# Three weight conversions tied to other marks, and one division moved to ScalarE, in a fused attention and FNet kernel

## The chip, the cores and the metric

The kernel runs on one core of a Trainium2 chip. TensorE (PE) multiplies, VectorE (DVE) and ScalarE (ACT) read its results from PSUM and write SBUF, GpSimd (POOL) helps a little, and SyncE (SP) issues nearly all the DMAs. The metric is the time on the device in microseconds (us), the median of several runs. One more execution was profiled; all rows below are from it.

## The reference

```
scores_l = scale * q @ k.T, masked to |i - j| < 16
scores_s = scale * q @ k_sum.T + log(32)       # k_sum: maxima over blocks of 32 keys
a = softmax(concat(scores_l, scores_s));  x = a @ concat(v, v_sum)   # v_sum: block means
x -> (4 batches, 768 tokens, 512 channels)
u  = x + real(fft2(x));   un = (u - mean) / sqrt(var + 1e-6)
out = u + relu(un @ w_ch1) @ w_ch2             # 512 -> 2048 -> 512
```

q, k, v have 4 batches, 8 heads, 768 tokens and 64 channels per head. The two weights arrive as float64, and the kernel turns them into float32 itself.

## The kernel before, in words

The four batches are worked one after the other, and the attention of batch b + 1 runs in the gaps of the two layers of batch b. Heads go in four pairs g = 0..3. For a pair, `scores` and `sum_scores` make the scores (tiles `sc`, `ss`) and their exponentials `p` on ScalarE; `values` multiplies them with the values into two PSUM banks `av`, whose last column is the sum of the exponentials, takes the reciprocal (`rec`), and multiplies the rest by it into `x` (for the tokens of batch 1 the tile is `x_919`, for those of batch 0 `x_145`). `prepare` transposes the next pair's q and k on TensorE (tiles `qk`) and ScalarE copies them out.

The two layers use a Strassen-like scheme: seven products instead of eight. `gen_hidden(b, c)` is the first layer, half c of the 16 column blocks: four steps j (0 to 3 for c = 0, 4 to 7 for c = 1), seven products each, in three banks `hx`, `hy`, `hz`, with left factors from a tile `w` of seven 128-column parts (four of the weight, three sums of them). Its result is the tile `h`. `gen_out(b, c)` is the second layer on that half: three rows i of token blocks, seven products each, in banks `ox`, `oy`, `oz`. VectorE adds every product to `x`; such an addition is a *join*. In `gen_out(0, 0)` the first row is done plainly: two tiles of 128 tokens (t = 0 and t = 3, banks `o`), one join each, while the right-hand sums of `w_ch2` (`w_0_0` to `w_0_3`) are still being formed.

`gen_weights` converts the weights during batch 0. One piece is one call of `make(f, j)`: f = 1 a column block of `w_ch1`, f = 2 a row block of `w_ch2`. The pieces go in the order of `plan`, and each piece's raw words are loaded into the tile `words`, which has room for two pieces. `convert` takes, on VectorE, five instructions of 128x1024 (exponent bits, mantissa bits, sign, scaled low word, product), on ScalarE two (exponent, mantissa), and then `_left_sums` or `_right_sums` adds three smaller ones on VectorE; the finished tile is stored to DRAM (`dw`) for the later batches. The third entry of a plan line is a stage. The generator goes on when this stage is in `issued`, and if `marks` has an instruction under that name, the piece's instructions are put behind that instruction by the scheduler (`tc.issue_after`). The stages `("h", 0, j)` are in `issued` only: they hold the generator back but name no instruction.

The order on each engine is set by a scheduler from the order of the code, its priorities and `issue_after`. PE, DVE, ACT and the DMA queue of SP each work through their own list.

Four PSUM banks serve `hx`..`oz` and `o`, and four more serve the attention. A product can start when the bank it gets has been read out by the join or the copy that used it last.

Of the kernel before, what the change touches and what calls it, by code (L numbers as in the profile page):

```python
# [12 lines left out]
AF = mybir.ActivationFunctionType  # L13
# [3 lines left out]
P = 128  # L17
# [479 lines left out]
def _main_program(ctx, tc, q, k, v, moe_w_ch1, moe_w_ch2, out):  # L497


    nc = tc.nc  # L500
    B, H, S, D = q.shape
    DM = H * D
    DF = moe_w_ch1.shape[1]
    NST = S // P
# [9 lines left out]
    HT = NST // 2  # L514
# [5 lines left out]
    ADD, SUB = ALU.add, ALU.subtract  # L520
# [39 lines left out]
    def fetch(out, in_):  # L560

        ins = nc.sync.dma_start(out=out, in_=in_)
        if in_order[0]:
            tc.keep_in_program_order(ins)
        return ins.ins

    def abank(shape, name):
        return psum.tile(shape, FP, tag="attn", bufs=4, name=name)

    def bank(shape, name):  # L570
        return psum.tile(shape, FP, tag="bank", bufs=4, name=name)
# [9 lines left out]
    def tt(out, in0, in1, op):  # L581
        return nc.vector.tensor_tensor(out=out, in0=in0, in1=in1, op=op).ins  # L582
# [5 lines left out]
    nat, marks = {}, {}  # L588
# [249 lines left out]
    def values(b, g, p, pm, x):  # L838
        vw = vw_bufs[g % 2]
        av = [abank([P, NST, D1], f"av_{b}_{g}_{r}") for r in range(2)]  # L840
        for t in range(NST):
            h = t // HT
            for j in range(4):
                for r in range(2):
                    rows, i = slice(64 * r, 64 * (r + 1)), 4 * t + j
                    nc.tensor.matmul(av[r][32 * j:32 * (j + 1), t, :], p[rows, h, i - NB2 * h, :], vw[rows, i, :],
                                     start=(t == 0), stop=False, skip_group_check=True)
        for t in range(HT):
            for r in range(2):
                rows = slice(64 * r, 64 * (r + 1))  # L850
                ins = nc.tensor.matmul(av[r][:, t:t + HT + 1:HT, :], pm[rows, P * t:P * (t + 1)], vs[rows],
                                       start=False, stop=(t == HT - 1), skip_group_check=True)
        marks["av", b, g] = ins.ins
        for r in range(2):
            rc = rec[:, b * NP + g, r]
            nc.vector.reciprocal(out=rc, in_=av[r][:, :, D])
            xo = x[:, 0, P * g + D * r:P * g + D * (r + 1)]
            xo = bass.AP(xo.tensor, xo.offset, [list(xo.ap[0]), [HT * DM + D * (1 - 2 * r), 2], [DM, HT], [1, D]])
            tt(xo, av[r].rearrange("p (h t) d -> p h t d", h=2)[:, :, :, 0:D],
               rc.rearrange("p (h t) -> p h t", h=2)[:, :, :, None].to_broadcast([P, 2, HT, D]), ALU.mult)  # L860
# [208 lines left out]
    def gen_attention(b):  # L1069
# [13 lines left out]
        for g in range(NP + 1):  # L1083
# [6 lines left out]
            if past:  # L1090
                if b > 1:
                    scale_sums(b, g - 1)
                values(b, g - 1, *past, x)
                if n1 and b > 1:
                    load_values(*n1)
# [50 lines left out]
    wt, issued = {}, set()  # L1146
# [1 line left out]


    plan = [(1, 0, ("fold", 0)), (1, 1, ("mx", 0)), (1, 2, ("mx", 0)), (2, 0, ("sums", 0)), (1, 3, ("h", 0, 0)), (2, 1, ("mx", 0)),  # L1150
            (2, 2, ("mx", 0)), (2, 3, ("mx", 0)), (1, 4, ("h", 0, 1)), (1, 5, ("h", 0, 2)), (1, 6, ("h", 0, 3)),
            (2, 4, ("o", 0, 0)), (1, 7, ("h", 0, 4))] + [(2, j, ("o", 0, 0)) for j in range(5, NJ)]
    pieces = [(f, j, hh) for f, j, _ in plan for hh in range(2)]
    raws, stores = [], []
# [354 lines left out]
    def one_sum(b, c, i):  # L1509

        if i and queue.get("last"):
            with tc.issue_after(marks["dense"]):
                for part in queue["last"].pop(0):
                    tt(*part)
# [192 lines left out]
    def gen_out(b, c):  # L1707
        x, h = x_of[b], wt["h", b]
        js = range(NC * c, NC * (c + 1))
        plain = (0, HT) if (b, c) == (0, 0) else ()  # L1710
        if plain:
            for t in plain:
                for j in js[0:2] if t == 0 else js[2:4]:
                    w = wt[2, 0, j]
                    tt(w[:, T1], w[:, B12], w[:, B11], SUB)
                    tt(w[:, T2], w[:, B22], w[:, T1], SUB)
                    tt(w[:, T4], w[:, B21], w[:, T2], SUB)
                ps = bank([P, DM], f"o_{b}_{c}_{t}")
                for n, j in enumerate(js):
                    for hf in range(2):  # L1720
                        nc.tensor.matmul(ps, h[:, n, hf, P * t:P * (t + 1)], wt[2, b, j][:, 2 * hf:2 * hf + 2, :],
                                         start=(n, hf) == (0, 0), stop=(n, hf) == (NC - 1, 1))
                    if n % 2 == 0:
                        yield
                tt(x[:, t, :], ps, x[:, t, :], ADD)
            for j in js:
                w = wt[2, 0, j]
                tt(w[:, T3], w[:, B22], w[:, B12], SUB)
                fetch(out=dw2[j][:, 1:7], in_=w[:, 1:7])
        for i in range(1 if plain else 0, HT):  # L1730
            t1, t2 = slice(P * i, P * (i + 1)), slice(S2 + P * i, S2 + P * (i + 1))
            left = {A11: h[:, :, 0, t1], A12: h[:, :, 1, t1], A22: h[:, :, 1, t2]}
            for s in (S1, S2_, S3, S4):
                left[s] = bpool.tile([P, NC, P], FP, tag="s", bufs=5, name=f"s{s}_{b}_{c}_{i}")
            a21 = h[:, :, 0, t2]
            tt(left[S1], a21, left[A22], ADD)
            tt(left[S2_], left[S1], left[A11], SUB)
            tt(left[S3], left[A11], a21, SUB)
            tt(left[S4], left[A12], left[S2_], SUB)
            X, Y, Z = (bank([P, HD], f"o{n}_{b}_{c}_{i}") for n in "xyz")  # L1740
            x11, x12 = x[:, i, 0:HD], x[:, i, HD:DM]
            x21, x22 = x[:, HT + i, 0:HD], x[:, HT + i, HD:DM]

            def product(ps, a, r, start, stop):
                for n, j in enumerate(js):
                    nc.tensor.matmul(ps, left[a][:, n, :], wt[2, b, j][:, r, :], start=start and n == 0,  # L1746
                                     stop=stop and n == NC - 1, skip_group_check=True)

            def join(*a):
                marks["dense"] = tt(*a)  # L1750
                if (b, c) == (B - 2, 1) and i:
                    joins.append(marks["dense"])

            product(X, A11, B11, True, False)
            join(x11, X, x11, ADD)
            product(Y, A12, B21, True, True)
            join(x11, Y, x11, ADD)
            one_sum(b, c, i)
            yield
            product(X, S2_, T2, False, False)  # L1760
            join(x12, X, x12, ADD)
            product(Z, S1, T1, True, False)
            join(x22, Z, x22, ADD)
            one_sum(b, c, i)
            yield
            product(X, S3, T3, False, False)
            join(x22, X, x22, ADD)
            last = (b, c, i) == (B - 1, 1, HT - 1)
            if last:
                fetch(out=out[b, P * (HT + i):P * (HT + i + 1), HD:DM], in_=x22)  # L1770
            product(Z, S4, B22, False, True)
            join(x12, Z, x12, ADD)
            if last:
                fetch(out=out[b, P * i:P * (i + 1), :], in_=x[:, i, :])
            one_sum(b, c, i)
            yield
            product(X, A22, T4, False, True)
            join(x21, X, x21, ADD)
            if NC * (c + 1) == NJ and not last:
                for t in (i, HT + i):  # L1780
                    fetch(out=out[b, P * t:P * (t + 1), :], in_=x[:, t, :])
            elif last:
                fetch(out=out[b, P * (HT + i):P * (HT + i + 1), 0:HD], in_=x21)
            if i == HT - 1:
                issued.add(("o", b, c))
            one_sum(b, c, i)
            yield
# [8 lines left out]
    ps = bank([P, 512], "warm")  # L1796
# [14 lines left out]
    for vw in vw_bufs + [third]:  # L1811
        nc.gpsimd.tensor_copy(out=vw[:, :, D].rearrange("p (e n) -> p e n", e=2),
                              in_=count[:, None, :].to_broadcast([P, 2, NQ]))
# [52 lines left out]
    for b in range(B):  # L1866
# [20 lines left out]
        if b == B - 2:  # L1887
# [9 lines left out]
            ps = bank([1, 1], "flag_ps")  # L1897
# [5 lines left out]
def kernel(tc, q, k, v, moe_w_ch1, moe_w_ch2, out):  # L1903
    nc = tc.nc
    with ExitStack() as ctx:
        flag = _main_program(ctx, tc, q, k, v, moe_w_ch1, moe_w_ch2, out)
        redo = nc.values_load(flag[0:1, 0:1], min_val=0, max_val=1)
    with tc.If(redo > 0):
        _general_program(tc, q, k, v, moe_w_ch1, moe_w_ch2, out)
# [30 lines left out]
```

## Time and profile before

| what | value |
|---|---|
| median of 3 runs | 794.03 us (792.45 to 794.19) |
| the profiled execution | 794.12 us, span 792.3 us |
| PE busy | 767.6 us (97%) |
| DVE busy | 541.1 us (68%) |
| ACT busy | 248.9 us (31%) |
| DMA | 120.36 MB, 152 GB/s mean |

Times in rows count from the start of the span. The profiled execution's time is 1.8 us more than its span, and 0.1 us above the median. Busy times of PE contain waiting inside its pipeline, so the waits, the clock and the distances between neighbouring rows say more than the share. Batch 0's layers, the conversions and batch 1's attention lie between about 86 and 240 us; after that the later batches follow.

### The profile page before, as it was taken

What the parts mean: (1) busy time and instruction counts of PE and PEld (TensorE: products, weight loads), DVE (VectorE), ACT (ScalarE), POOL (GpSimd) and SP (SyncE); (2) the same over time, 40 slices, a digit from 0 to 9 for tenths busy, and PEclk for the clock granted to TensorE, in tenths of its full rate; (3) what the DMA queues carried; (4) which work ended last, traced back from release to release, by engine and by line L of the source; (5) the groups of instructions that cost most, each with busy time, mean ns of one, the idle gap of its engine ahead of it and who ended that gap; (6) DMA issues with size and microseconds to landing.
All of it is one profiled execution on the core that took longest, in us unless ns stands there. A gap on an engine that the chain in (4) does not pass through costs nothing.

```text
span 792.3 us, 14996 instructions
## 1 busy us (share of the span) xinstructions
PE 767.6 (97%) x6068; PEld 591.0 (75%) x6068; DVE 541.1 (68%) x1145; ACT 248.9 (31%) x579; POOL 74.3 (9%) x102
## 2 busy tenths in 40 slices
PE   8999999869999999999999999999999999999997
PEld 5777555557569876688669876688659889889986
DVE  4789999976988825464576726463476987756762
ACT  3755657232535212200126112210116214203300
POOL 1000000000000002300030002300030004201500
PEclk8999999969999999999999999999999999999999
DMA  9897879695884359966244149820614034204001
GB/s 201 227 247 176 182 239 259 204 271 195 223 220 143 92 172 244 182 97 161 93 183 153 41 147 200 220 95 27 251 48 156 27 145 188 93 1 186 0 29 57
DMA packets 135901, 120.36 MB, mean 152 GB/s; under 512 B 94512, under 2 KB 117904, under 8 KB 135824
## 3 DMA queue, kind: packets, MB, share of 16 engines
q1 hardware_dynamic: 134672, 117.05, 53.6%
q0 software_dynamic: 576, 2.10, 0.8%
q8 instruction: 50, 0.82, 0.4%
q10 hardware_dynamic: 576, 0.17, 0.1%
q14 instruction: 27, 0.22, 0.1%
HBM read 97.28 MB, written 22.02 MB: 151 GB/s over the span
## 4 chain that ended last, share of the span: by engine, by line
PE 80%; DVE 12%; ACT 3%; DMA 2%; issue 1%; SPq 0%; DVEq 0%
PE ox L1746 19%; PE hx L1450 13%; PE oz L1746 10%; PE hz L1450 6%; PE oy L1746 5%; PE t L1619 4%; PE hy L1450 3%; PE y L1323 3%; DVE w L582 2%; PE f L1619 2%; PE mx L1282 2%; DMA words<-in_moe_w_ch_dram 2%; PE sc L810 2%; DVE w L1192 2%; PE sc L750 1%
## 5 line engine op out<-in xcount | busy, mean ns | idle before, releaser
L1450 PE MATMUL hx<-u,w 128*128 128x384 f32 x384 | 139.8, 492 | 1.2 <-ACT h L1461 0.8
L1450 PEld LDWEIGHTS hx<-u,w 128*128 128x128 f32 x384 | 71.1, 190 | 52.9 <-ACT p L817 3.7
L1746 PE MATMUL ox<-w,h 128*128 128x256 f32 x368 | 87.5, 382 | 4.1 <-DVE x L582 4.1
L1746 PE MATMUL ox<-w,s 128*128 128x256 f32 x368 | 89.3, 385 | 0.0
L1746 PE MATMUL oz<-w,s 128*128 128x256 f32 x368 | 89.0, 380 | 0.0
L1746 PEld LDWEIGHTS ox<-w,h 128*128 128x128 f32 x368 | 69.5, 191 | 16.1 <-DVE x L582 4.3
L1746 PEld LDWEIGHTS ox<-w,s 128*128 128x128 f32 x368 | 70.2, 193 | 10.6 <-DVE x L582 0.8
L582 DVE TENSOR_TENSOR x<-ox,x 128x256 f32<-128x256 f32 x92 | 38.9, 423 | 56.3 <-PE ox L1746 56.0
L1746 PEld LDWEIGHTS oz<-w,s 128*128 128x128 f32 x368 | 69.6, 190 | 9.5 <-DVE x L582 0.4
L1450 PE MATMUL hz<-u,w 128*128 128x384 f32 x192 | 70.3, 488 | 0.1
L1450 PEld LDWEIGHTS hz<-u,w 128*128 128x128 f32 x192 | 36.4, 190 | 25.6 <-DVE u L582 0.7
L1461 ACT COPY h<-hx 128x384 f32<-128x384 f32 x24 | 11.4, 476 | 114.0 <-PE hx L1450 114.0
L1746 PE MATMUL oy<-w,h 128*128 128x256 f32 x184 | 44.3, 381 | 0.7 <-ACT h L1668 0.7
L1622 ACT COPY f<-t 128x192 f32<-128x192 f32 x52 | 15.8, 303 | 78.3 <-PE t L1619 78.1
L582 DVE TENSOR_TENSOR x<-oz,x 128x256 f32<-128x256 f32 x46 | 19.5, 423 | 29.4 <-PE oz L1746 29.1
L1746 PEld LDWEIGHTS oy<-w,h 128*128 128x128 f32 x184 | 34.7, 190 | 6.2 <-ACT h L1668 1.5
L1598 POOL TENSOR_SCALAR h<-h 128x768 f32<-128x768 f32 x12 | 25.4, 2127 | 137.5 <-DVE h L1578 137.5
L585 POOL TENSOR_TENSOR vb<-vb 96x512 f32<-96x512 f32 (+2 forms) x20 | 20.4, 1022 | 174.2 <-DMA vb<-in_v_dram 173.2
L1450 PE MATMUL hy<-u,w 128*128 128x384 f32 x96 | 35.2, 488 | 1.5 <-DVE h L582 1.5
L582 DVE TENSOR_TENSOR s<-h 128x512 f32<-128x512 f32 x46 | 31.4, 682 | 0.9 <-ACT h L1458 0.6
L1477 ACT ACTIVATE h<-hx 128x384 f32<-128x384 f32 x24 | 11.7, 489 | 61.9 <-PE hx L1450 61.9
L582 DVE TENSOR_TENSOR h<-hy,h 128x384 f32<-128x384 f32 x24 | 13.3, 556 | 25.7 <-PE hy L1450 25.6
(236 smaller groups left out, 1310.5 us busy)
## 6 DMA issues: line engine op xcount, KB each, us to landing
w<-dw SPq DMA_DIRECT2D x46, 896.0 KB, 6.0
words<-in_moe_w_ch_dram SPq DMA_DIRECT2D x32, 512.0 KB, 6.0
dw<-w SPq DMA_DIRECT2D x12, 896.0 KB, 7.8
vw<-in_v_dram SPq DMA_DIRECT2D x47, 192.0 KB, 5.8
out_dram<-x SPq DMA_DIRECT2D x23, 256.0 KB, 2.0
vb<-in_v_dram SPq DMA_DIRECT2D x24, 192.0 KB, 8.1
kn<-in_k_dram SPq DMA_DIRECT2D x9, 384.0 KB, 6.4
qn<-in_q_dram SPq DMA_DIRECT2D x9, 384.0 KB, 7.2
```

What stands on the lines that cost most here:

```text
L582: return nc.vector.tensor_tensor(out=out, in0=in0, in1=in1, op=op).ins
L585: return nc.gpsimd.tensor_tensor(out=out, in0=in0, in1=in1, op=op).ins
L810: ins = nc.tensor.matmul(ps[h][r:r + 64, i, :], kt[rows, o:o + 64], qt[rows, o:o + BLOCK], start=True, stop=True)
L1192: nc.vector.scalar_tensor_tensor(out=dst, in0=low, scalar=2.0 ** -52, in1=dst, op0=ALU.mult, op1=ALU.add)
L1282: nc.tensor.matmul(out, y[:, g], table, start=False, stop=True, skip_group_check=True)
L1323: nc.tensor.matmul(y, fgs[b][par][:, st, P * g:P * (g + 1)], fs[par][:, g % 2, st, :], start=(st == 0), stop=(st == n - 1))
L1450: ins = nc.tensor.matmul(ps, w[:, a, kk, :], u[:, r, kk, :], start=start and kk == 0, stop=stop and kk == 1, skip_group_check=True)
L1477: nc.scalar.activation(out=c21, in_=X, func=AF.Relu)
L1598: nc.gpsimd.tensor_scalar(out=t, in0=t, scalar1=0.0, scalar2=None, op0=ALU.max)
L1619: marks["two"] = nc.tensor.matmul(o, left(j, a, m), rhs(r, m), start=m in (1, 5), stop=m in (2, 3, 4, 5, 7), skip_group_check=True).ins
L1622: nc.scalar.copy(out={1: f[:, 0], 6: f[:, 1], 7: g}[m], in_=t)
L1746: nc.tensor.matmul(ps, left[a][:, n, :], wt[2, b, j][:, r, :], start=start and n == 0, stop=stop and n == NC - 1, skip_group_check=True)
```

## The change

Two edits. First, three lines of `plan` get other stages: the blocks j = 4, 5 and 6 of `w_ch1`, which waited for `("h", 0, 1)`, `("h", 0, 2)` and `("h", 0, 3)`, now wait for `("row", 0)`, `("row", 1)` and `("row", 2)`. These are new marks, each a real instruction: the join of the first plain tile (t = 0), and the second join of rows i = 1 and i = 2 in `gen_out(0, 0)`. The conversions' instructions are put behind them. Second, for batch 1 and pairs g = 2 and 3, the multiplication by the reciprocal, one VectorE instruction of 128x384 per bank, becomes six ScalarE instructions of 128x64 per bank (24 in all).

```diff
             rc = rec[:, b * NP + g, r]
             nc.vector.reciprocal(out=rc, in_=av[r][:, :, D])
+            if b == 1 and g > 1:
+                for t in range(NST):
+                    c = P * g + D * (r ^ (t // HT))
+                    nc.scalar.activation(out=x[:, t, c:c + D], in_=av[r][:, t, 0:D], func=AF.Identity, scale=rc[:, t:t + 1])
+                continue
...
     plan = [(1, 0, ("fold", 0)), (1, 1, ("mx", 0)), (1, 2, ("mx", 0)), (2, 0, ("sums", 0)), (1, 3, ("h", 0, 0)), (2, 1, ("mx", 0)),
-            (2, 2, ("mx", 0)), (2, 3, ("mx", 0)), (1, 4, ("h", 0, 1)), (1, 5, ("h", 0, 2)), (1, 6, ("h", 0, 3)),
+            (2, 2, ("mx", 0)), (2, 3, ("mx", 0)), (1, 4, ("row", 0)), (1, 5, ("row", 1)), (1, 6, ("row", 2)),
             (2, 4, ("o", 0, 0)), (1, 7, ("h", 0, 4))] + [(2, j, ("o", 0, 0)) for j in range(5, NJ)]
...
+        def pace(i, ins):
+            if ("row", i) not in issued:
+                marks["row", i] = ins
+                issued.add(("row", i))
...
-                tt(x[:, t, :], ps, x[:, t, :], ADD)
+                pace(0, tt(x[:, t, :], ps, x[:, t, :], ADD))
...
             product(Y, A12, B21, True, True)
             join(x11, Y, x11, ADD)
+            if plain:
+                pace(i, marks["dense"])
```

The instructions stand differently in the lists. In the names, `w_0_4_..`, `w_0_5_..` and `w_0_6_..` with 128x1024 rows are the pieces of `w_ch1`; `words` are raw words; `o_0_3` is the plain tile t = 3; `ox_0_1` is the bank `ox` of batch 0, row i = 1. Line numbers of the changed kernel are 5 higher around `plan` and 11 higher in `gen_out`.

DVE before, from the final product of w1 block 4 on to the first join of row 1 (most of blocks 5 and 6 stand between, cut here):

```order
L582 TENSOR_TENSOR w_0_4_1538<-w_0_4_1538,words 128x1024
L1187 TENSOR_SCALAR w_0_5_1593<-words 128x1024
...
L582 TENSOR_TENSOR w_0_6_1632<-w_0_6_1632,words 128x1024
L582 TENSOR_TENSOR x_919<-av_2_0_1646,rec 128x2x3x64
L856 RECIPROCAL rec<-av_2_1_1647 128x6
L582 TENSOR_TENSOR w_0_6_1632<-w_0_6_1632 128x256
L582 TENSOR_TENSOR x_919<-av_2_1_1647,rec 128x2x3x64
L582 TENSOR_TENSOR w_0_6_1632<-w_0_6_1632 128x2x256
L582 TENSOR_TENSOR x_145<-o_0_3_1629,x_145 128x512
```

DVE now, at the same place:

```order
L582 TENSOR_TENSOR w_0_4_1604<-w_0_4_1604,words 128x1024
L856 RECIPROCAL rec<-av_2_1_1619 128x6
L582 TENSOR_TENSOR w_0_4_1604<-w_0_4_1604 128x256
L582 TENSOR_TENSOR x_145<-o_0_3_1601,x_145 128x512
L582 TENSOR_TENSOR w_0_4_1604<-w_0_4_1604 128x2x256
L582 TENSOR_TENSOR w_0_3_1504<-w_0_3_1504 128x256
L582 TENSOR_TENSOR w_0_4_1604<-w_0_4_1604 128x256
L582 TENSOR_TENSOR x_145<-ox_0_1_1710,x_145 128x256
L582 TENSOR_TENSOR x_145<-oy_0_1_1711,x_145 128x256
L1192 TENSOR_SCALAR w_0_5_1724<-words 128x1024
```

The join of the plain tile t = 3 stood 22 rows behind the product of block 4 and stands 3 rows behind it now; block 5 comes after row 1's second join, block 6 after row 2's.

PE before, behind the third product of row 1 (`sc_3` are the scores of batch 1's last pair, 24 rows of 64x32, `qk` the transposes for batch 2; rows left out where the dots are):

```order
L1746 MATMUL oz_0_1_1730<-w_0_3_1504,s_0_0_1_1720 128x256
L810 MATMUL sc_3_0_1788<-qt_3_1554,kt_81 64x32 x2
...
L828 MATMUL ss_3_1843<-qt_3_1554,km_83 32x384 x4
L710 MATMUL qk_0_0_1912<-ident,kn_0_1233 128x128 x3
...
L834 MATMUL vs_3_1937<-vbs_1_1237,sel 128x64
L1746 MATMUL ox_0_2_1775<-w_0_0_1250,h_0_1255 128x256
L1746 MATMUL ox_0_1_1728<-w_0_0_1250,s_0_0_1_1721 128x256
```

PE now, from the same product on:

```order
L1757 MATMUL oz_0_1_1712<-w_0_3_1504,s_0_0_1_1702 128x256
L1757 MATMUL ox_0_1_1710<-w_0_0_1250,s_0_0_1_1703 128x256
...
L1757 MATMUL oy_0_2_1772<-w_0_3_1504,h_0_1255 128x256
L810 MATMUL sc_3_0_1789<-qt_3_1544,kt_81 64x32 x2
...
L828 MATMUL ss_3_1844<-qt_3_1544,km_83 32x384 x4
L1757 MATMUL ox_0_2_1771<-w_0_0_1250,s_0_0_2_1764 128x256
```

Row 1's last four products and row 2's first two now stand ahead of the scores, and the transposes `qk` (and `vs_3`) have gone further down, into step j = 4 of the first layer.

SP's DMA list before, after the load of block 5's words:

```order
L562 DMA dw_2_97<-w_0_2_1415 128x256
L562 DMA dw_3_98<-w_0_3_1504 128x256
L562 DMA dw_0_95<-w_0_0_1250 128x1536
L562 DMA words<-in_moe_w_ch_dram 128x4x256 x2
L562 DMA dw_1_96<-w_0_1_1382 128x1536
```

SP's DMA list now:

```order
L562 DMA dw_0_95<-w_0_0_1250 128x1536
L562 DMA dw_1_96<-w_0_1_1382 128x1536
L562 DMA dw_2_97<-w_0_2_1415 128x1536
L562 DMA dw_3_98<-w_0_3_1504 128x1536
L562 DMA dw_2_97<-w_0_2_1415 128x256
L562 DMA words<-in_moe_w_ch_dram 128x4x256 x2
```

The load of block 6's words stands behind four stores of 128x1536 instead of one; the last of these waits for the last right-hand sum of `w_0_3`, a VectorE instruction in the second fence above.

## The prediction

> **What bounds the kernel now.** I read the page first, then the stretch of the two layers of batch 0 in windows, then its timeline for each engine.
>
> ```profile
> span 792.3 us, 14996 instructions
> PE 767.6 (97%) x6068; PEld 591.0 (75%) x6068; DVE 541.1 (68%) x1145; ACT 248.9 (31%) x579; POOL 74.3 (9%) x102
> PE   8999999869999999999999999999999999999997
> PEclk8999999969999999999999999999999999999999
> ...
> PE 80%; DVE 12%; ACT 3%; DMA 2%; issue 1%; SPq 0%; DVEq 0%
> ```
>
> PE is the bound nearly everywhere. The one deep notch is slice 9 of 40 (158 to 178 us), in PE's busy row and in its clock. The windows show who fills it (columns: PE, weight loads, DVE, ACT, POOL, granted clock, DMA share, GB/s):
>
> ```profile
> 150.00:160.00 10.00, 6.50 (x124) 4.81 (x123) 10.00 (x15) 4.92 (x6) 0.00 (x0) 0.94 0.80 226
> 160.00:170.00 10.00, 4.85 (x14) 2.97 (x15) 8.14 (x16) 6.20 (x13) 0.00 (x0) 0.50 0.84 274
> 170.00:180.00 10.00, 10.00 (x42) 8.57 (x42) 6.92 (x13) 0.00 (x0) 0.00 (x0) 0.87 1.07 303
> 180.00:190.00 10.00, 10.00 (x48) 8.73 (x47) 4.76 (x9) 1.84 (x2) 0.00 (x0) 1.00 0.38 125
> ...
> 189.70:229.70 40.00, 38.79 (x221) 22.78 (x220) 33.69 (x52) 20.23 (x35) 0.00 (x0) 1.00 0.80 225
> ```
>
> DVE is full while PE starves, and half idle 20 us later. PE's timeline:
>
> ```profile
> 148.30 1.89 PE L1746 MATMUL ox<-w,h 128*128 128x256 f32 x8
> ...
> 151.75 1.89 PE L1746 MATMUL oz<-w,s 128*128 128x256 f32 x8
> 153.57 1.60 PE L810 MATMUL sc<-qt,kt 64*64 64x32 f32 x96
> 155.75 0.85 PE L828 MATMUL ss<-qt,km 64*32 64x384 f32 x8 [0.58 <-ACT p L817]
> 156.53 0.55 PE L710 MATMUL qk<-ident,kn 128*128 128x128 f32 x3
> 160.68 0.90 PE L710 MATMUL qk<-ident,kn 128*128 128x128 f32 x3 [3.60 <-ACT p L829]
> 163.72 0.69 PE L834 MATMUL vs<-vbs,sel 96*128 96x64 f32 x2
> 168.55 1.22 PE L1746 MATMUL ox<-w,h 128*128 128x256 f32 x2 [4.13 <-DVE x L582]
> 169.56 3.44 PE L1746 MATMUL ox<-w,s 128*128 128x256 f32 x8
> ...
> 182.77 1.89 PE L1746 MATMUL oz<-w,s 128*128 128x256 f32 x8
> 184.49 1.89 PE L1746 MATMUL ox<-w,s 128*128 128x256 f32 x8
> ```
>
> One product of the second layer takes 1.73 us from start to start (182.77 to 184.49), so the third product of row 1 ends at 153.5. From there to 168.55 PE does only attention work, and waits at the end for a bank that the join of the plain tile t = 3 frees. DVE's own rows say why that join is late:
>
> ```profile
> 146.21 0.70 DVE L1174 TENSOR_SCALAR words<-words 128x1024 int32<-128x1024 int32 x1
> 146.81 0.70 DVE L1187 TENSOR_SCALAR w<-words 128x1024 int32<-128x1024 int32 x1
> ...
> 152.14 0.69 DVE L1187 TENSOR_SCALAR w<-words 128x1024 int32<-128x1024 int32 x1
> ...
> 164.13 0.69 DVE L1174 TENSOR_SCALAR words<-words 128x1024 int32<-128x1024 int32 x1 [1.86 <-DMA words<-in_moe_w_ch_dram]
> ...
> 166.74 0.55 DVE L582 TENSOR_TENSOR x<-av,rec 128x384 f32<-128x384 f32 x1
> ...
> 167.81 0.69 DVE L582 TENSOR_TENSOR x<-o,x 128x512 f32<-128x512 f32 x1
> ```
>
> The tile's last product was done before 148.30, where row 1's first product starts, yet the join runs at 167.81, behind the conversions of w1 blocks 4, 5 and 6, one of which waits 1.86 us for its words. One DVE instruction starts about 0.08 to 0.10 before its predecessor's end (146.21 to 146.81 for 0.70).
>
> **What the notch costs.** From 153.5 to 168.55 are 15.05 us. The work in it would take at full clock: scores 1.5, `ss` 0.8 (155.75 to 156.53), the twelve transposes 1.3 and `vs` 0.1, together 3.7. The 1.3 is from the same transposes 28 us earlier, below. So 11.4 us are lost. Then the clock: the eight passes of a product take 3.44 at 169.56 and 1.73 later. From 168.55 to the first layer's second half at 189.67 are 21.1 us for eleven products of 1.73, 19.0: 2.1 lost, so about 4.2 us were at half clock. In the second half itself:
>
> ```profile
> 128.32 0.82 PE L710 MATMUL qk<-ident,kn 128*128 128x128 f32 x6
> 129.63 0.81 PE L1450 MATMUL hx<-u,w 128*128 128x384 f32 x2
> ...
> 189.67 1.45 PE L1450 MATMUL hx<-u,w 128*128 128x384 f32 x4
> 190.96 1.45 PE L1450 MATMUL hy<-u,w 128*128 128x384 f32 x4
> ...
> 206.54 1.20 PE L846 MATMUL av<-vw,p 64*32 64x65 f32 x96
> 208.54 2.85 PE L1450 MATMUL hx<-u,w 128*128 128x384 f32 x8
> ...
> 213.43 0.91 PE L1450 MATMUL hx<-u,w 128*128 128x384 f32 x2 [0.75 <-ACT h L1461]
> ...
> 229.74 1.89 PE L1746 MATMUL ox<-w,h 128*128 128x256 f32 x8
> ```
>
> 28 products of 1.29 (189.67 to 190.96) are 36.1, the value products 2.0 (206.54 to 208.54); the stretch lasts 40.1, so 2.0 are lost. In all 15.5 us between 153.5 and 229.74: that is the most that better order there can bring.
>
> **The change part by part.** Nothing of the conversions goes away. Moved: with the t = 3 join three rows behind block 4's product, it and row 1's two joins come early. Before 152.14 DVE's list is as it was. Then come a reciprocal (0.1), a sum (0.34), the join (0.6), a sum of two parts (0.6), two sums (0.7): the first `ox` join runs from 154.5 to 154.95. PE stands ready at about 153.6: a wait of 1.4 remains, where 11.4 was. Rows 1 and 2 then run at full clock, since PE never stands still for 3.6 us as it did before 160.68.
>
> What the move makes late are the conversions, and who waits for them. I followed the new lists with the durations of before, an instruction starting when its queue and its inputs are ready. The waits that PE then meets:
>
> First, `ss_3` needs a bank that the exponentials free. On ACT these now stand behind block 6's mantissa, which waits for DVE behind row 2's second join (at 166.0). 0.6 on DVE, 1.04 on ACT and 0.45 for one exponential end at 168.2; the scores end at 166.95. A wait of 1.3.
>
> Second, the transposes `qk`, now in step j = 4, bring eight copies on ACT:
>
> ```profile
> 129.50 2.06 ACT L713 COPY kt<-qk 64x384 f32<-64x384 f32 x4
> 131.59 2.11 ACT L713 COPY qt<-qk 64x384 f32<-64x384 f32 x4
> ...
> 151.12 1.15 ACT L1175 ACTIVATE words<-words,rebias 128x1024 int32<-128x1024 int32 x1 [2.09 <-DVE words L1174]
> ...
> 45.49 1.33 ACT L798 ACTIVATE x<-av,rec 128x64 f32<-128x64 f32 x6 [0.83 <-DVE rec L792]
> ```
>
> The copies take 4.2 us, `vs_3` needs the sixth, and PE has 1.3 of other work: a wait of 2.1. Behind the copies two evictions of step 5 come late, 0.9.
>
> Third, the division. Six ACT instructions of 128x64 take 1.33 (the row from batch 0 above); four groups are 5.3, and four DVE instructions of 0.55 go, of which DVE gets back 1.9. Pair g = 2's groups fall on 149 to 154, where ACT idles 2.09 us once (151.12) and nobody waits for the result; I cost them nothing. If that cover fails, block 5's mantissa is up to 2.7 later, and DVE with it. Pair g = 3's two groups stand in step 6 ahead of the copy of `hx`: with what follows, 1.8 on PE.
>
> New waits: 1.4 + 1.3 + 2.1 + 0.9 + 1.8 = 7.5. Gain: 15.5 - 7.5 = 8.0.
>
> [...]
>
> DMA: the load of block 6's words is moved past three stores of 768 KB, behind the last sum of `w_0_3` on DVE (154.6). It is issued at 154.8 and needed at 162.8; the later loads (blocks 4 to 7) have 7 to 8 us each too. From issue to landing took, for the words from 145 to 215 us and from 20 to 240 us:
>
> ```profile
> DMA to landing us min/median/max: 3.5/5.7/7.6
> DMA to landing us min/median/max: 3.5/6.0/14.1
> ```
>
> At the median none of them is late, at 7.6 the last costs less than 1 us, so I put 0 in the sum and take 14.1 as the other end.
>
> Behind 229.74 the lists of PE, DVE and ACT are as before, the inputs of the next batch do not come from this stretch, and PE is full (the page's slices), so the gain should stay.
>
> **The sum.** The profiled execution took 794.12 us with a span of 792.3, 0.1 above the median of 794.03. 794.1 - 8.0 = 786.1. The lower bound has only the first two new waits (2.7): 781.3. The upper bound is with the rivals.
>
> **The rivals.** (a) The waits in the first layer's second half do not arise, because ACT's copies fit between; speaks for it that before lost only 2.0 there: 781.3. (b) DVE and ACT are the bound there: from 189.7 to 229.74 DVE has 33.7 of 40 busy even before, and the same work now meets a PE that comes 12 us earlier. One more wait of 1 us per step, as the 0.75 at 213.43 once before, makes 4: 790.1. (c) The words come late by queueing behind the four stores. In the order of the lists DVE then stands at the next `words` row with the joins behind it. Landing at 10 us costs some 5.4; and a stop over 3.6 us would halve the clock again as at 160 to 170, 2.1 more: 786.1 + 7.5 = 793.6, no change. (d) Slower: the same mechanism with 12 us per load. Beyond 9 to 10 every further microsecond is paid by block 6's, 7's and the last row blocks' loads in turn, about 3 for 1. Gain and loss meet at 11; at 12 the second half ends 3.4 later than before: 797.5. The 14.1 speaks for it, the 7.6 of this stretch against it.
>
> [...]
>
> (e) That the change does nothing is excluded by the lists: the t = 3 join stands elsewhere.
>
> **How the numbers follow.** 0.2% is 1.6 us, about what a measurement of this kernel tells from none. Forecast 786.1 (own range 784 to 788.5) 0.50; (a) 0.14; (b) 0.18; (c) 0.07; (d) 0.11. Faster is forecast, (a) and (b): 0.82; the same (c): 0.07; slower (d): 0.11. The range 781.3 to 790.5 takes in forecast, (a) and (b), leaving out 0.18.
>
> **What would show it.** The step from `oz` of row 1 to the next product is about 1.4 us instead of 15; the granted clock stays 1.00 from 150 to 180; the first half's rows end near 177.6 where they ended at 189.67, and the second layer's second half starts near 221.7, not 229.74. A wait of PE on ACT of about 2 us at the `qk` copies shows the second term, one before `hx` of step 6 the third. I am wrong if DVE shows waits for `words` of several microseconds, if a slice with half clock is left, or if the time saved there is given back before 260.

## The result, and the profile after

The changed kernel takes 780.82 us (median of 4 runs, 778.93 to 781.79), the kernel before, with one more run of it, 793.24 (4 runs, 791.03 to 794.19). The ratio is 0.9844, 95% interval 0.9813 to 0.9876. The prediction was faster, 786.1, with a range from 781.3 to 790.5: the direction was right, and the time lies 0.5 us below the range. A second series with more runs gave 781.41 (6 runs) against 792.23 (23 runs), ratio 0.9875 [0.9855, 0.9895], so 9.9 us less [8.3, 11.5].

The head of the page after:

```profile
span 777.1 us, 15014 instructions
PE 760.5 (98%) x6068; PEld 585.0 (75%) x6068; DVE 538.9 (69%) x1141; ACT 253.4 (33%) x603; POOL 74.5 (10%) x102
PE   8999999999999999999999999999999999999997
PEclk9999999999999999999999999999999999999999
...
PE 78%; DVE 13%; ACT 4%; DMA 3%; issue 1%; SPq 0%; DVEq 0%
```

The notch of slice 9 is gone from PE's row and from its clock. The same stretch in windows (columns as before: PE, weight loads, DVE, ACT, POOL, granted clock, DMA share, GB/s):

```profile
150.00:160.00 10.00, 10.00 (x47) 8.81 (x47) 9.89 (x18) 2.21 (x2) 0.00 (x0) 1.00 1.03 323
160.00:170.00 10.00, 9.88 (x138) 7.59 (x137) 9.30 (x16) 3.35 (x5) 0.00 (x0) 1.00 0.97 210
170.00:180.00 10.00, 9.97 (x42) 6.76 (x43) 7.98 (x13) 5.16 (x9) 0.00 (x0) 1.00 0.92 303
180.00:190.00 10.00, 9.04 (x32) 4.93 (x32) 8.16 (x11) 9.04 (x18) 0.00 (x0) 1.00 0.47 170
```

DVE is as full as before, but now PE is full beside it. PE's timeline after:

```profile
143.16 1.89 PE L1757 MATMUL ox<-w,h 128*128 128x256 f32 x8
...
146.62 1.89 PE L1757 MATMUL oz<-w,s 128*128 128x256 f32 x8
149.80 1.99 PE L1757 MATMUL ox<-w,s 128*128 128x256 f32 x8 [1.30 <-DVE x L582]
...
160.36 1.60 PE L810 MATMUL sc<-qt,kt 64*64 64x32 f32 x96
161.89 0.85 PE L828 MATMUL ss<-qt,km 64*32 64x384 f32 x8
162.67 1.99 PE L1757 MATMUL ox<-w,s 128*128 128x256 f32 x8
...
171.86 1.45 PE L1455 MATMUL hx<-u,w 128*128 128x384 f32 x4
...
178.33 1.46 PE L1455 MATMUL hx<-u,w 128*128 128x384 f32 x4
179.74 0.43 PE L834 MATMUL vs<-vbs,sel 96*128 96x64 f32 x2
180.01 1.51 PE L1455 MATMUL hz<-u,w 128*128 128x384 f32 x4
...
185.23 0.81 PE L1455 MATMUL hz<-u,w 128*128 128x384 f32 x2
186.95 1.56 PE L1455 MATMUL hx<-u,w 128*128 128x384 f32 x4 [0.92 <-ACT h L1466]
...
198.13 1.45 PE L1455 MATMUL hz<-u,w 128*128 128x384 f32 x4
200.29 1.56 PE L1455 MATMUL hx<-u,w 128*128 128x384 f32 x4 [0.72 <-ACT h L1466]
...
214.62 1.89 PE L1757 MATMUL ox<-w,h 128*128 128x256 f32 x8
```

Two marks are used from here on, since both are the same work in every kernel: the first `ox` of row 1 (143.16 here, 148.30 before), and the first `ox` of the second layer's second half (214.62, before 229.74). Between them lies the *stretch*: 71.46 us after, 81.44 before, so 9.98 less. What stands behind the second mark is the same: 777.1 - 214.62 = 562.5, before 792.3 - 229.74 = 562.6 (562.5 to 563.8 in all runs below but e10_warm). But the first mark, too, is 5.1 us earlier after, though up to about there PE's list is the same in both kernels. The windows from the start say most of why, first before, then after:

```profile
0.00:20.00 20.00, 16.87 (x136) 10.78 (x136) 9.69 (x28) 7.21 (x14) 2.06 (x11) 0.83 1.01 202
```

```profile
0.00:20.00 20.00, 17.15 (x176) 10.66 (x176) 12.56 (x32) 10.38 (x21) 2.07 (x11) 1.00 1.05 204
```

The granted clock of the first 20 us was 0.83 in the profiled execution before and 1.00 in the one after (136 against 176 PE instructions done). PE's first 48 `av` products begin at 23.92 before and at 20.45 after, so 3.5 of the 5.1 us are lost by then; the rest goes with a pause of 1.30 us that PE makes at 40.1 before. So of the 15.2 us between the two spans, about 10.0 belong to the change and 5.1 to the start of these two executions; the first series of runs tests that.

### The profile page after: what moved, and what is told of

It reads as the page before. It is cut to its first block, busy times and chain, and to the rows that moved or that the text cites. A ratio compares the mean times of both kernels' runs of the same rounds, so it can differ in the third digit from the quotient of the medians.

```text
span 777.1 us, 15014 instructions
## 1 busy us (share of the span) xinstructions
PE 760.5 (98%) x6068; PEld 585.0 (75%) x6068; DVE 538.9 (69%) x1141; ACT 253.4 (33%) x603; POOL 74.5 (10%) x102
## 4 chain that ended last, share of the span: by engine, by line
PE 78%; DVE 13%; ACT 4%; DMA 3%; issue 1%; SPq 0%; DVEq 0%
PE ox L1757 18%; PE hx L1455 13%; PE oz L1757 9%; PE hz L1455 6%; PE oy L1757 5%; PE t L1624 4%; PE y L1328 3%; PE hy L1455 3%; DVE w L582 3%; PE f L1624 2%; PE mx L1287 2%; DVE w L1197 2%; PE sc L810 2%; DVE words L1195 1%; DMA dw<-w 1%; DVE x L582 1%
```

## The experiments

Of each run the table gives the two marks of its profiled execution, the stretch between them, the span, and the timing. The rows from e4_before to e3_div, from e7_gate to e10_warm, and from e13_wide on are three series; each has its own runs of the kernel before (17 to 23).

| kernel | marks, us | stretch | span | median, us | ratio to before |
|---|---|---|---|---|---|
| before | 148.30, 229.74 | 81.44 | 792.3 | 793.24 (4) | |
| after | 143.16, 214.62 | 71.46 | 777.1 | 780.82 (4) | 0.9844 [0.9813, 0.9876] |
| e4_before (before again) | 144.51, 225.74 | 81.23 | 788.2 | 791.96 (12) | 1.0000 [0.9983, 1.0018] |
| e1_after (after again) | 147.12, 218.90 | 71.78 | 782.0 | 781.41 (6) | 0.9875 [0.9855, 0.9895] |
| e2_plan (marks alone) | 146.57, 217.78 | 71.21 | 780.6 | 782.47 (6) | 0.9887 [0.9866, 0.9907] |
| e3_div (division alone) | 145.91, 227.22 | 81.31 | 790.3 | 790.26 (12) | 0.9986 [0.9972, 1.0001] |
| e7_gate | 149.07, 220.07 | 71.00 | 782.7 | 780.74 (6) | 0.9860 [0.9830, 0.9890] |
| e5_row0 | 144.81, 216.39 | 71.58 | 778.9 | 780.74 (5) | 0.9858 [0.9826, 0.9890] |
| e9_row0b | 145.60, 215.42 | 69.82 | 778.0 | 781.53 (5) | 0.9858 [0.9823, 0.9892] |
| e10_warm | 145.32, 229.73 | 84.41 | 796.2 | 796.53 (12) | 1.0049 [1.0026, 1.0072] |
| e13_wide | 146.25, 225.69 | 79.44 | 788.4 | 789.91 (12) | 0.9969 [0.9954, 0.9985] |
| e11_obank | 146.68, 227.97 | 81.29 | 791.0 | 790.52 (12) | 0.9985 [0.9963, 1.0007] |
| e6_row12 | 144.80, 215.84 | 71.04 | 779.0 | 780.20 (4) | 0.9851 [0.9820, 0.9883] |
| e12_best | 145.00, 214.91 | 69.91 | 778.7 | 779.07 (5) | 0.9837 [0.9810, 0.9863] |

Theory A: the hole of 15 us was the join of t = 3 behind three conversions; the ties bring it forward, and that is the gain, all of it in the stretch. Rival B: the kernel after is faster from its start on, as the first pair of profiles seems to say. Theory C: the division counts as much as the marks.

**Both kernels again (e4_before, e1_after).** No edit. The expectations of this first series count from the end of row 1's third product, 5.2 us behind the first mark: their 66 and 76 us are the 71.46 and 81.44 of the table less 5.2.

> The kernel before once more, unaltered, as a control. Theory A: ratio 1.000 within 0.3%, the stretch 76 us, and the start part anywhere from 148 to 154 us according to the clock in the first 20 us. Rival B: the start part is 153.5 again.

> The changed kernel once more, unaltered. Theory A (the gain lies between the third product of row 1 and the second half of the second layer, and what the profiled pair differs by ahead of it is the start-up clock of single executions): that stretch lasts 66 us again (76 before), everything behind it 562.5 us, and the time from the start to that product (148.4 here, 153.5 before) varies by some microseconds with the clock granted in the first 20 us; ratio 0.983 to 0.988. Rival B (the changed kernel is faster from its start on, by 4 to 5 us): the start part is 148.4 again whatever the clock, and the ratio is 0.981 or less.

The stretches repeat within 0.3 us (81.44 and 81.23; 71.46 and 71.78). The first mark does not: 144.51 and 147.12, where the first pair had 148.30 and 143.16, the other way round. So the earlier start of the first pair was no effect of the change, and rival B falls: over all runs the first mark lies at 144.5 to 148.3 in the six traces with the old `plan` and at 143.2 to 149.1 in the eight with new marks. The change is worth 9.7 us by the mean stretches (81.34 - 71.62).

**The parts alone (e2_plan, e3_div).**

```
e2_plan = after without
-            if b == 1 and g > 1:
-                for t in range(NST):
...
e3_div = before with these lines, the plan lines as before
```

> The three marks alone; the division stays on VectorE. Theory A: the notch goes with the marks, so most of the gain is here: stretch 67 to 69 us, gain 9 to 11 of the 12. Theory C (the division matters as much, since ScalarE frees the two value banks at 148 to 149 and the scores of the last pair take them without waiting): the scores wait for a bank until VectorE has divided, the stretch is 71 us or more and the gain 6 or less.

> The division on ScalarE alone; the stages as before. Theory A: the join of the plain tile still stands behind the conversions of blocks 5 and 6, so a wait of PE of 10 us or more with half clock is still there; gain 0 to 1.5 us. Theory C: banks come free earlier, the transposes and scores no longer wait 3.6 us for one, the clock does not drop, and the gain is 3 us or more.

PE's timeline of the marks alone, then of the division alone:

```profile
146.57 1.89 PE L1752 MATMUL ox<-w,h 128*128 128x256 f32 x8
...
202.19 1.56 PE L1450 MATMUL hx<-u,w 128*128 128x384 f32 x4 [0.78 <-ACT h L1461]
```

```profile
152.72 0.85 PE L828 MATMUL ss<-qt,km 64*32 64x384 f32 x8
...
158.81 0.90 PE L710 MATMUL qk<-ident,qn 128*128 128x128 f32 x3 [4.08 <-ACT kt L713]
...
164.96 3.78 PE L1757 MATMUL ox<-w,h 128*128 128x256 f32 x8 [4.42 <-DVE x L582]
```

The marks alone bring the whole gain in the stretch (71.21, or 66.0 in the terms of the expectation, which had 67 to 69). With the division alone the hole stays, with its two waits and the slow products behind it (3.78 for eight passes), and the stretch is 81.31. Its ratio of 0.9986 has an interval that reaches 1.0001: no gain is shown, and C falls. The rows at 152.72 and 202.19 matter below: with the division moved, `ss` no longer waits as it did before (0.58 at 155.75), and the wait before `hx` of step 6 is there with the division on DVE, too (0.78).

**Which tie, and what of it (e5_row0, e6_row12, e7_gate).**

```
e5_row0:  (1, 4, ("row", 0)), (1, 5, ("h", 0, 2)), (1, 6, ("h", 0, 3))
e6_row12: (1, 4, ("h", 0, 1)), (1, 5, ("row", 1)), (1, 6, ("row", 2))
e7_gate:  -                marks["row", i] = ins
```

> Only block 4's conversion is tied (to the first plain join); blocks 5 and 6 are back on their old stages. In DVE's list the join of t = 3 already stands three rows behind block 4's product. Theory A (one release suffices to take the 15 us hole away, since the hole is one join behind three conversions): stretch 72 to 75 us, ratio 0.988 to 0.992, granted clock 1.00 from 150 to 180. Rival (each of the three ties takes a third of the hole, about 3.3 us each): stretch near 78, ratio near 0.996.

> The change with block 4's conversion back on its old stage; only blocks 5 and 6 are tied to the joins of rows 1 and 2. In DVE's list the join of t = 3 stands three rows behind block 4's product here too. Theory A (any one release suffices): stretch 71 to 72, ratio 0.986 to 0.988, like the run in which only block 4 was tied. Rival (block 4's tie is the one that counts): stretch 75 or more.

> The change, but the marks only hold the conversions' turn back in the order of the program; the explicit edge that puts a block's conversion behind its join is left out. Theory A (it is the order of DVE's queue alone that counts; DVE's list differs from the change's in 13 rows, ACT's and the DMA list in none): from row 1's first ox to the second half's first ox 71.5 us as with the change (before: 81.3), ratio 0.987 to 0.989. Rival (the explicit edge is what keeps the joins ahead): the hole comes back in part, 74 us or more in the stretch, ratio above 0.991.

Stretches of 71.58 (e5_row0), 71.04 (e6_row12) and 71.00 (e7_gate). Block 4's tie alone takes the whole hole away, a little more fully than I had expected (72 to 75), and so do those of blocks 5 and 6 without it; block 5's or block 6's alone was not run. Three shares of 3.3 us are excluded. Nor is the explicit edge needed: to hold the generator back until the join has been emitted is enough. The ties change PE's list along with DVE's, as the lists under The change show, and no run changes the one without the other.

**Another bank for the second plain tile (e11_obank).** The conversions stay in front of the joins, but the product that waited at 168.55 before no longer waits for that tile's bank. By PE's list this is row 2's first product; the expectation calls it row 1's third accumulator, which had its bank at 151.75.

```
-                ps = bank([P, DM], f"o_{b}_{c}_{t}")
+                ps = (abank if t else bank)([P, DM], f"o_{b}_{c}_{t}")
```

> The kernel before, with the second plain tile (t = 3) put into a bank of the attention's pool, so that row 1's third accumulator need not wait for that tile's join. Conversions stay where they were. Theory A (the late joins are the hole, whichever bank is asked for first): row 1's next products find a bank, but the joins of row 1 still stand behind the conversions, so PE stops one or two products later; the hole shrinks by at most 4 us, stretch 77 to 81. Rival (the one held bank is the hole): stretch 71 to 73, as with the change.

```profile
146.68 1.89 PE L1746 MATMUL ox<-w,h 128*128 128x256 f32 x8
...
151.86 1.89 PE L1746 MATMUL ox<-w,h 128*128 128x256 f32 x8
...
166.04 0.90 PE L710 MATMUL qk<-ident,kn 128*128 128x128 f32 x3 [4.50 <-DVE x L582]
...
165.44 0.55 DVE L582 TENSOR_TENSOR x<-av,rec 128x384 f32<-128x384 f32 x1
```

One product more is done at once (151.86). Then the attention, which has a bank less, waits 4.50 us. What it waits for is the division of pair 2 on DVE (the last row, 165.44 to 165.99), which reads out a value bank and stands behind the conversions as well. The stretch is 81.29, nothing gained; my upper end was 81. The order on DVE makes the hole, whichever bank is asked for first.

**The half clock by itself (e10_warm, e13_wide).** Both are the kernel before with filling work in PE's second idle part; its results are not used.

```
e10_warm
-        nc.tensor.matmul(ps, pick, vb, start=True, stop=True)
+        for _ in range(18 if (b, g) == (1, NP - 1) else 1):
+            nc.tensor.matmul(ps, pick, vb, start=True, stop=True)
e13_wide, behind the same matmul, in a larger tile pw of the same bank
+        for _ in range(6 if wide else 0):
+            nc.tensor.matmul(pw[:, P:S2], ident, near[:, 0]...[:, 0:2 * P], start=True, stop=True)
```

> The kernel before, with the last vs product of batch 1 repeated 18 times into the same bank (same values), so that PE has work during the second half of its hole (about 163.7 to 168). The hole itself stays. Theory A (about 2 of the 10 us are the halved clock that follows the hole, and work in it restores it): the first products behind the hole take 1.7 instead of 3.4 us, stretch 79 to 80 instead of 81.3, ratio 0.9975. Rival (the slow clock is covered, since DVE's joins set the pace behind the hole anyway): the products take 1.7, but the stretch stays at 81.3, ratio 1.000. Third: the repeats end after the join, stretch 81.3 plus their overhang.

> The kernel before, with six wide products (128x128 by 128x256, full precision, results not used) behind the last vs product of batch 1, in PE's second idle part of the hole. The 18 narrow repeats (64 columns) of the run before did not bring the clock back: PE was busy from 157.7 to 168.4 us and the granted clock stayed 0.50. Theory N (only wide work counts towards the return of the clock): the clock comes back some 4 to 5 us after the wide work begins, at about 166, the first ox behind the hole takes 1.9 instead of 3.4 us, and the stretch is 79.5 to 80 (before 81.3), ratio about 0.998. Rival (the clock returns a fixed time after the hole's end, whatever fills it): the products behind stay at 3.4 us, the stretch stays at 81.3 or grows by the overhang.

The narrow filling first (timeline, then the window), then the wide one:

```profile
160.71 7.94 PE L835 MATMUL vs<-vbs,sel 96*128 96x64 f32 x36
168.44 2.87 PE L1747 MATMUL ox<-w,h 128*128 128x256 f32 x6
...
160.00:170.00 10.00, 9.88 (x43) 9.21 (x42) 7.56 (x16) 3.29 (x7) 0.00 (x0) 0.50 0.84 278
```

```profile
162.15 3.90 PE L838 MATMUL vs<-near,ident 128*128 128x256 f32 x12
166.84 1.56 PE L1750 MATMUL ox<-w,h 128*128 128x256 f32 x6 [0.79 <-DVE x L582]
168.24 1.89 PE L1750 MATMUL ox<-w,s 128*128 128x256 f32 x8
```

With 64 columns PE counts as 9.88 of 10 us busy, and the clock stays at 0.50; the filling overran the join, and the kernel lost 3.1 us in the stretch (the third case). Behind its second mark the profiled execution lost another 3.9 (566.5): PE waits 2.11 us for POOL at 305.35, and the clock is at 0.50 for 3.4 us from 306.6 on. With 256 columns the products behind the hole run at full speed, and the stretch is 79.44, 1.9 less than before, ratio 0.9969 [0.9954, 0.9985]. So the half clock behind the hole was a term of its own of about 2 us, as the prediction had it (2.1), and about 8 of the 9.7 are the idle time.

**A later mark (e9_row0b), and without the division (e12_best).**

```
-                pace(0, tt(x[:, t, :], ps, x[:, t, :], ADD))
+                ins = tt(x[:, t, :], ps, x[:, t, :], ADD)
+                if t:
+                    pace(0, ins)
e12_best: the same, division on DVE as before
```

> The change, but block 4's conversion is tied to the second plain join (t = 3) instead of the first, so that this join stands ahead of it. The change left a wait of PE for that join of 1.30 us at row 1's third step. Theory A (the wait is only the place of that join in DVE's queue): it shrinks to under 0.5, stretch 70.5 to 71, about 0.5 to 1 us faster than the change (ratio to before 0.986). Rival (DVE is the bound of this stretch, what is taken from this wait comes back at the next one that waits for DVE): stretch 71.5 as with the change, ratio 0.9875.

> Block 4's conversion tied to the second plain join, blocks 5 and 6 to rows 1 and 2 as in the change, and the division back on DVE. The run with the division on ScalarE had a stretch of 69.8 and the wait of 1.3 us was gone. If the division is worth nothing (theory A): stretch 69.5 to 70.5, ratio 0.985 to 0.987, and the wait of 0.7 for the eviction at step 6 stays. If it pays once the joins are early (DVE is full from 150 to 170): stretch 71 or more.

```profile
145.60 1.89 PE L1759 MATMUL ox<-w,h 128*128 128x256 f32 x8
...
149.06 1.89 PE L1759 MATMUL ox<-w,s 128*128 128x256 f32 x8
...
201.09 1.56 PE L1455 MATMUL hx<-u,w 128*128 128x384 f32 x4 [0.72 <-ACT h L1466]
```

```profile
201.78 1.56 PE L1450 MATMUL hx<-u,w 128*128 128x384 f32 x4 [0.42 <-ACT h L1466]
```

Row 1 now goes on without a wait, and the stretch is 69.82, 1.6 to 2.0 less than with the change, where 0.5 to 1 was expected. It stays so without the division (69.91); step 6 waits 0.42 instead of 0.72 (0.7 was expected), and row 2 waits 0.40 for a join instead of 0.17. e12_best has the lowest ratio of all, 0.9837 [0.9810, 0.9863], but its interval meets that of e1_after, and its profiled execution is 1.3 us longer than the changed kernel's behind the second mark (563.8 against 562.5). So both are faster than the change in the stretch only; that either beats it in time is not shown.

## Why the prediction was right in direction and wrong in size

The measured 780.82 is 5.3 us below 786.1. Of these 1.7 to 2.0 are the gain itself (9.7 by the mean stretches, 9.98 in the first pair, against 8.0), 1.9 the base, and some 1.5 the spread between runs (792.2 - 9.7 = 782.5; all ten runs of the changed kernel have a median of 781.4). The larger gain alone, 794.1 - 9.98 = 784.1, would have stayed in the range; the base and the spread put the time below it. Two things failed, then: two of the five new waits, 3.4 of the 7.5 us, did not come, and a third came at half its price; and the sum stood on one execution with a late start.

**The base.** "The profiled execution took 794.12 us": the sum was made against this one execution. Its start had the slow clock (0.83, the row above), and 23 runs put the kernel before at 792.23. The prediction looked only at the stretch of the notch; the first windows of the same trace, with the clock at 0.83, would have told of a late start. The first mark lay between 143.2 and 149.1 us in the fourteen profiled executions, though the work up to there hardly differs.

**The hole, 15.5 us at most.** Right, in each part: the join behind the conversions is the hole (e2_plan, e5_row0, e6_row12 without it; e3_div and e11_obank with it), and 2 of it are clock (e13_wide). The new place of the join was right too. With the 5.14 us of the earlier start added back, the first half's rows end at 177.0 (177.6 was forecast) and the second layer's second half starts at 219.8 (221.7): most of what the forecast missed lies in the first layer's second half. DVE's rows after:

```profile
147.46 0.68 DVE L582 TENSOR_TENSOR x<-o,x 128x512 f32<-128x512 f32 x1
...
149.33 0.42 DVE L582 TENSOR_TENSOR x<-ox,x 128x256 f32<-128x256 f32 x1
...
163.01 0.69 DVE L1179 TENSOR_SCALAR words<-words 128x1024 int32<-128x1024 int32 x1 [0.38 <-DMA words<-in_moe_w_ch_dram]
```

The `ox` join starts 6.17 us after row 1's first product (149.33 - 143.16); 154.5 was forecast, 6.2 after 148.30.

**The first wait, 1.4.** Measured 1.45: `oz` at 146.62 plus 1.73 is 148.35, and the next product starts at 149.80.

**The second, 1.3 for `ss_3`: 0.** `ss` follows `sc` at once (161.89). This step failed. It had `ss` wait for a bank that the exponentials free, but they start later than `ss` itself. The step has what the rows before show, where `ss` does wait 0.58 for the exponentials (155.75), and where DVE divides pair 2, and so reads out its two value banks, only at 165.87 and 166.74, behind the conversions. After, ACT has read them out by 148.56 (the row at 147.22), so `ss` finds a bank. In e3_div, where the division alone is moved and the first value bank is read out by 147.87, the wait of 0.58 is gone too; in e2_plan DVE divides by 151.83 and `ss` follows `sc` at once at 165.17. Which bank `ss` gets, the rows do not name. ACT's rows after:

```profile
147.22 1.34 ACT L860 ACTIVATE x<-av,rec 128x64 f32<-128x64 f32 x6
...
162.49 0.85 ACT L817 ACTIVATE p<-sc 128x384 f32<-128x384 f32 x2
...
178.65 2.08 ACT L713 COPY kt<-qk 64x384 f32<-64x384 f32 x4
180.76 2.06 ACT L713 COPY qt<-qk 64x384 f32<-64x384 f32 x4
...
196.94 2.55 ACT L860 ACTIVATE x<-av,rec 128x64 f32<-128x64 f32 x12
```

**The third, 2.1 for `vs_3`: about 0.1.** It failed in the same way: the rows before gave the bank. There `vs` starts at 163.72, 0.05 behind the end of the sixth copy (the second of `qt`, from 162.66 on at 0.51 each). After, it starts at 179.74, 0.05 behind the second of the eight copies (0.52 each from 178.65), and in e2_plan and e12_best about as much behind the second. A product takes 1.29 from 178.33, so at most 0.12 us were lost. Both steps used the banks of the order before for an order in which others were free.

**Step 5, 0.9.** Measured 1.07: two passes of `hz` from 185.23 end at 185.88 (0.65, half of 1.29), and `hx` starts at 186.95.

**The division in step 6, 1.8.** Measured 0.87 (198.13 + 1.29 = 199.42, next at 200.29), and PE's wait is there without the division as well: 0.72 with it and 0.78 in e2_plan, 0.72 in e9_row0b and 0.42 in e12_best. So the division itself costs between nothing and 0.3 there. Without it the copy of `hx` stands behind other work: in e2_plan behind the mantissa of a conversion on ACT, from 200.72 to 201.78. The wait before `hx` of step 6, which was to show the third term, thus came for another reason as well. The division's price on ACT was right: six take 1.28 (half of 2.55; before 1.33). What failed is that the step put all of it on PE's path.

**The sum of the waits.** 7.5 were forecast. The five terms measured 1.45 + 0 + 0.1 + 1.07 + 0.87 = 3.5. The stretch says that 15.5 - 9.98 = 5.5 were lost in all; the other 2.0 are small steps of up to 0.3 between kinds of products, which no term named.

**The rivals.** By the time, (a) with 781.3 came nearest, but only through the base: by the gain, 9.7 to 10.0 stands nearer to the forecast's 8.0 than to the 12.8 of (a). Its point that ACT's copies fit between was right. (b) did not come: DVE is 93 to 99% busy from 150 to 170 and PE meets two waits in the second half, not four. (c) and (d) did not come: DVE waited 0.38 us for `words`. The clock stayed at 1.00 in the windows from 150 to 190, as forecast to 180. That it takes a stop as long as the 3.6 us before 160.68 to lower it, as (c) and the step for rows 1 and 2 have it, is not borne out by the other runs (last section).

## What to carry to other kernels

When an engine starves beside a full one, look in the full one's list for a short instruction that frees something and stands behind long ones that nobody waits for; here it was enough to hold back one block of them, and two other blocks did as well. Sum only the removed wait with confidence; a new wait that rests on which buffer is handed out, or on a queue that was late anyway, deserves a chance, not its full price: ask first which buffers the new order has freed by then. Before a forecast is set against one profiled execution, compare it with others from a common mark: here the way to the first mark alone differed by up to 6 us. The clock column does not tell all of it: e7_gate has the latest mark, 149.07, with 1.00 in its first 20 us, though six transposes took 1.54 us there (at 13.96) and 0.88 in the first execution after (at 10.46).

## What the runs showed of the hardware

How long the clock stayed slow. Windows of 1 us around the beginning and the end of the slow clock, for the kernel before, for e10_warm and for e13_wide:

```profile
158.00:159.00 1.00, 0.00 (x0) 0.00 (x0) 1.00 (x4) 0.84 (x1) 0.00 (x0) 0.94 0.60 113
172.00:173.00 1.00, 1.00 (x5) 0.86 (x4) 0.83 (x1) 0.00 (x0) 0.00 (x0) 0.73 0.72 155
```

```profile
156.00:157.00 1.00, 0.00 (x0) 0.00 (x0) 1.00 (x3) 1.00 (x2) 0.00 (x0) 0.70 0.92 258
173.00:174.00 1.00, 1.00 (x5) 0.84 (x4) 0.00 (x0) 0.00 (x0) 0.00 (x0) 0.77 1.09 339
```

```profile
157.00:158.00 1.00, 0.00 (x0) 0.00 (x0) 1.00 (x3) 1.00 (x2) 0.00 (x0) 0.77 0.86 233
164.00:165.00 1.00, 1.00 (x5) 0.87 (x4) 1.00 (x4) 0.81 (x2) 0.00 (x0) 0.82 1.10 306
```

Between them the windows show 0.50, so a mean of 0.94 in a window of 1 us means that the clock fell 0.88 into it. So it was slow from 158.88 to 172.54, from 156.40 to 173.46, and from 157.54 to 164.36: 13.66, 17.06 and 6.82 us. Nearer the start of the kernel before it was slow from 8.70 to 15.52 (0.85 in the window from 8 to 9, 0.74 from 15 to 16), 6.82 again. The shortest spell was 3.4 us, in e4_before (0.66 from 75 to 80). These five lengths are near 4, 5, 2, 2 and 1 times the shortest; why, no run shows. The prediction's estimate for the kernel before, about 4.2 us at half clock once the products went on at 168.55, was near the 3.99 measured there (to 172.54), but the time is not the same in every run: in e13_wide it took 2.2 us from the first wide product (162.15).

Nor did it take a wait of 3.6 us to bring the clock down, as the prediction had it. Before, PE's last transpose ended at 157.08 (156.53 + 0.55) and the clock fell at 158.88, 1.8 us into the wait of 3.60. In e11_obank it fell at 159.62 behind waits of 0.59 and 1.60 (at 155.86 and 159.05), in e1_after at 99.0 behind one of 1.49 (mean clock 0.97 from 83 to 140), in e10_warm at 306.6 behind one of 2.11. The same wait of 1.49 left the clock at 1.00 in the trace before (at 101.30), and so did one of 1.30 after (at 149.80). What decides between them was not shown.

Not all work that the busy column counts brought the clock back. In e10_warm PE had products of 64 columns from 160.71 to 168.44, with weight loads in 9.21 of the 10 us from 160 to 170, and the clock stayed at 0.50 all that time. It stayed there for another 5.0 us, with products of 256 columns from 168.44 on, and came back at 173.46. In e13_wide it came back 2.2 us behind the first of the wide products, as said above. Whether it is the columns, or the share of weight loads, was not tried.
